# A linear-recurrence layer with two gated MLPs: the causal mask of the key products goes from VectorE to GpSimd, the low half of the receptance products from GpSimd to VectorE, and the instruction order is planned anew

## The chip, the core and the metric

One core of one Trainium2 chip runs the whole program. The time is that of one execution in microseconds (us) on the device; 1069.03 us is the median of three runs of the kernel before.

## What is computed

The reference has three parts, one behind the other. With 4 sequences, 8 heads, 768 steps and a head width of 40, each head keeps a 40x40 state:

```
for t in range(S):
    y[:, :, t] = einsum('bhd,bhde->bhe', r_t, state)
    Sa = einsum('bhde,bhe->bhd', state, a_t)
    state = state * w_t[:, :, None, :] - einsum('bhd,bhe->bhde', Sa, b_t)
    state = state + einsum('bhd,bhe->bhde', v_t, k_t)
x = y as 3072 tokens of 320
h = x @ w_in (320x2048);   g = h where h >= 1, 0 where h <= -1, else (h+1)**2/4;   x = g @ w_out
x = (silu(x @ w_gate) * (x @ w_val)) @ w_out2          (320x1536, then back to 320)
```

All inputs are float32.

## The kernel before

**Chunks.** Time is cut into 12 chunks of 64 steps. Within a chunk the recurrence is written as matrix products, one "pass" for each of the 4 sequences, so there are 48 passes. Float32 values are carried as a float16 high part and a float16 low part (value minus high part), and the products of the parts are added up in PSUM.

**A pass in front** (`p_tasks`, independent of the state): keys and receptances are scaled with the decays, split into parts (`kbs`, `ars`), turned, and multiplied at L889 (`pg`, 128 partitions x 512, the key products). The upper 64 partitions are masked causally by VectorE at L895 (PSUM times a 0/1 `mask`, into the SBUF tile `gf` for chunks 2 to 11, in place in PSUM for chunks 0 and 1), the lower 64 are copied by ScalarE at L899. From `gf` come `lkt` (high part ScalarE L910, low part GpSimd L916) and `l21` (L912, L570).

**The inverse** (`inv_tasks`, one for each chunk): 62 steps on VectorE in pairs (L955, L960), in a `pg` slot of PSUM.

**A pass behind** (`m_tasks`, needs the state of the chunk before): products at L1086, L1097, L1104, a turn by DMA, then the receptance products at L1165 into `pg`. VectorE masks them at L1171 into the SBUF tile `qf` (chunks 1 to 11), ScalarE casts the high part at L1175 into `wt`, GpSimd subtracts for the low part (helper `split`, L570). L1189 uses `wt` for y and the new state; L1195, L1198 and a DMA turn make the state of the next chunk, and L1222 makes the chunk's y, which goes by DMA to the MLPs.

**The MLPs.** For each chunk (256 tokens) layer 1 runs 8 pieces of L1234 (`ph`), ScalarE L1266/L1267, VectorE L1270, cast L1254, GpSimd low part L570, and L1301 (`po`); layer 2 runs 6 pieces with gate and value (L1234, L1281, L1284) and L1301. The weights are read during the first third in 58 pieces; VectorE takes the bits apart in three rows for each (L644, L648, L654).

**The order.** Every operation is a task with an engine, a cost and a due time. A planner (`Plan.forward`, `Plan.backward`) places the tasks in a list for each engine; engines work through their lists in order. Tables of numbers for each chunk and each step shift the due times. PSUM `pg` has two slots, shared by key products, receptance products, y and the inverse; `gf` and `qf` have one slot each. A task that writes a tile is placed only once the planner has a slot for it.

Of the kernel before, what the change touches and what calls it, by code (L numbers as in the profile page):

```python
# [8 lines left out]
F32 = mybir.dt.float32  # L9
# [3 lines left out]
ALU = mybir.AluOpType  # L13


class Plan:
# [10 lines left out]
    def __init__(self):  # L27
        self.tasks, self.made, self.pools, self.slots = [], {}, {}, {}
        self.bias, self.unit, self.nudge, self.last = 0.0, ["z", 0, 0], ({}, {}), ({}, {})
        self.lim, self.rounds, self.loose = 1.13, 4, ()  # L30
# [38 lines left out]
    def forward(self, prio):  # L69
# [59 lines left out]
        while done < len(ts):  # L129
            started = True  # L130
            while started:
                started = False
                for eng in self.ENGINES[:5]:
# [7 lines left out]
                    while any(heaps):  # L141
# [42 lines left out]
                        if t["dma"]:  # L184
                            heapq.heappush(events, (end, -1))
                            dma = max(dma, begin) + t["dma"]
                            end = dma + 1.94
                        else:
                            end += t["lat"]
# [30 lines left out]
    def backward(self, prio):  # L220
# [16 lines left out]
        def lat(t):  # L237
            return 1.44 + t["dma"] if t["dma"] else t["lat"]
# [107 lines left out]
def tile_recurrence__then__gated_mlps(  # L346
# [40 lines left out]
    WTP = range(1, 12)  # L387
# [63 lines left out]
    sbt("qf", [128, H, C], F32, 1)  # L451
# [83 lines left out]
    def c_v(n, ps=False):  # L535
        return 0.15 + n * 1.04e-3
# [19 lines left out]
    def hc(ap):  # L556
        return ap.rearrange("p (h t) -> p h t", h=H)
# [266 lines left out]
    def p_tasks(n, p):  # L824
# [61 lines left out]
        def mm():  # L886
# [8 lines left out]
        T("DVE", c_v(512, True), lambda: v_.tensor_tensor(  # L895
            out=gm(), in0=hc(G("pg", key))[0:C],
            in1=mask[0:C].unsqueeze(1).to_broadcast([C, H, C]), op=ALU.mult),
          r=[(key, "g")], w=[(key, "gm")], use=PG + GM, p=p)
        T("ACT", c_s(512), lambda: s_.activation(  # L899
            out=G("gf", key)[C:128], in_=hc(G("pg", key))[C:128], func=AF.Copy, scale=2.0**-6),  # L900
          r=[(key, "g")], w=[(key, "gf")], use=PG + GF, p=p)

# [114 lines left out]
    def m_tasks(n, p):  # L1017
# [144 lines left out]
        def mm_q():  # L1162
# [5 lines left out]
        wtp = c in WTP  # L1168
        qm = lambda: G("qf", key) if wtp else hc(G(pg, (key, "q")))
        QM = [("qf", key)] if wtp else PQ  # L1170
        T("DVE", c_v(512, True), lambda: v_.tensor_tensor(  # L1171
            out=qm(), in0=hc(G(pg, (key, "q"))),
            in1=mask.unsqueeze(1).to_broadcast([128, H, C]), op=ALU.mult),
          r=[(key, "q")], w=[(key, "pf")], use=PQ + QM, p=p)
        T("ACT", c_s(512), lambda: s_.copy(out=G("wt", key)[:, 0, :, 0:C], in_=qm()),  # L1175
          r=[(key, "pf")], w=[(key, "ph")], use=QM + WT, p=p)
        e4, eng, cost = side(wtp, 512)
        T(eng, cost, lambda: split(G("wt", key)[:, 1, :, 0:C], qm(), 1.0, G("wt", key)[:, 0, :, 0:C], e4),
          r=[(key, "ph")], w=[(key, "wt")], use=QM + WT, p=p)

# [160 lines left out]
    def by(tables):  # L1341
# [3 lines left out]
        "a": {0: 0.7, 11: -0.75},  # L1345
        "b": {3: 0.07, 5: -0.15, 7: 1.48, 8: -0.07, 10: 2.42, 11: 7.11},
        "d": {0: 5.17, 1: 4.15, 2: 3.13},
        "i": {0: -2.35, 1: -1.77, 2: -1.74, 3: -0.61, 4: 2.98, 6: 1.13, 7: 3.24, 8: 2.28, 9: 3.28, 10:
            7.81, 11: 4.67},
        "o": {0: 49.18},  # L1350
        "p": {15: 0.02, 16: 0.55, 17: 0.02, 18: 0.02, 19: 0.02, 20: 0.02},
        "v": {3: 0.77, 16: 0.81, 17: 0.81},
        "w": {0: 0.8, 1: 0.03, 2: -0.74, 3: -1.52, 4: -2.29, 5: -3.06, 6: -3.84, 7: -4.61},
        "z": {0: 16.32},
    })
    by_step = by({
# [37 lines left out]
    })  # L1394
    by_step = by({
# [179 lines left out]
```

## Time and profile before

| | |
|---|---|
| median of three runs | 1069.03 us (1068.96 to 1069.24) |
| profiled execution, its own time | 1068.32 us |
| its span, first to last instruction | 1066.6 us |
| mean granted TensorE clock | 0.978 of full |
| busy: TensorE / VectorE / ScalarE / GpSimd | 881.3 / 683.1 / 734.7 / 812.0 us |

The own time is 1.7 us above the span, and the median 0.7 us above that. A busy share is a mean over stages: before the MLPs start TensorE is mostly idle, and behind that it is hardly ever idle. So stages have to be read one by one. In the rows PE is TensorE, DVE VectorE, ACT ScalarE, POOL GpSimd.

### The profile page before, as it was taken

What the parts mean: (1) busy time and instruction counts of PE and PEld (TensorE: products, weight loads), DVE (VectorE), ACT (ScalarE), POOL (GpSimd) and SP (SyncE); (2) the same over time, 40 slices, a digit from 0 to 9 for tenths busy, and PEclk for the clock granted to TensorE, in tenths of its full rate; (3) what the DMA queues carried; (4) which work ended last, traced back from release to release, by engine and by line L of the source; (5) the groups of instructions that cost most, each with busy time, mean ns of one, the idle gap of its engine ahead of it and who ended that gap; (6) DMA issues with size and microseconds to landing.
All of it is one profiled execution on the core that took longest, in us unless ns stands there. A gap on an engine that the chain in (4) does not pass through costs nothing. (4 is left out here: it accounts for less than half of the span.)

```text
span 1066.6 us, 28811 instructions
## 1 busy us (share of the span) xinstructions
PE 881.3 (83%) x10944; PEld 730.6 (68%) x10944; DVE 683.1 (64%) x1773; ACT 734.7 (69%) x1358; POOL 812.0 (76%) x1040
## 2 busy tenths in 40 slices
PE   0322233947976999999999999999999999999998
PEld 0321232826754788888888878888888888888887
DVE  8879996896798475684855937648459467431211
ACT  1787575867976886978769779687697774653422
POOL 4589788877889799998998989999898785542221
PEclk9999999967988999999999999999999999999999
DMA  7987777688897689787768785887758454120000
GB/s 226 217 199 205 205 175 165 156 181 195 169 239 174 132 147 152 140 157 149 146 132 164 126 164 116 155 169 155 133 116 161 87 110 75 49 49 16 15 1 26
DMA packets 386195, 147.94 MB, mean 139 GB/s; under 512 B 344536, under 2 KB 362776, under 8 KB 386056
## 3 DMA queue, kind: packets, MB, share of 16 engines
q1 hardware_dynamic: 364756, 137.70, 61.1%
q10 hardware_dynamic: 21300, 8.40, 3.9%
q8 instruction: 85, 1.39, 0.6%
q14 instruction: 54, 0.44, 0.1%
HBM read 78.25 MB, written 21.52 MB: 94 GB/s over the span
## 5 line engine op out<-in xcount | busy, mean ns | idle before, releaser
L1301 PE MATMUL po<-wo,mx 128*128 128x320 f16 x2016 | 310.8, 300 | 4.2 <-POOL wo L570 2.2
L570 POOL TENSOR_TENSOR mx<-mx 128x512 f16<-128x512 f32 x168 | 194.1, 1159 | 109.9 <-ACT mx L1254 104.0
L1301 PEld LDWEIGHTS <-mx 128*128 128x128 f16 x2016 | 190.3, 98 | 71.3 <-issue 4.5
L1234 PE MATMUL ph<-mx,w 128*128 128x256 f16 x1536 | 194.1, 277 | 6.3 <-DMA mx<-x 3.5
L1234 PEld LDWEIGHTS <-w 128*128 128x128 f16 x1536 | 148.3, 99 | 29.6 <-issue 7.2
L1234 PE MATMUL ph<-x2t,wg 128*128 128x256 f16 x1152 | 142.8, 275 | 2.8 <-POOL wg L570 1.4
L1270 DVE SCALAR_TENSOR_TENSOR mx<-ph,mx 128x512 f32<-128x512 f32 x96 | 66.2, 689 | 123.2 <-ACT mx L1267 123.0
L1234 PE MATMUL ph<-x2t,wv 128*128 128x256 f16 x1152 | 141.7, 274 | 3.9 <-DVE wv L572 3.9
L1254 ACT CAST mx<-mx 128x512 f16<-128x512 f32 x168 | 102.7, 613 | 61.3 <-DVE mx L1284 31.6
L1234 PEld LDWEIGHTS <-wg 128*128 128x128 f16 x1152 | 110.5, 98 | 19.0 <-POOL wg L570 1.9
L1234 PEld LDWEIGHTS <-wv 128*128 128x128 f16 x1152 | 110.9, 98 | 18.2 <-DVE wv L572 4.2
L960 DVE TENSOR_TENSOR pg<-pg,ub 128x126 f32<-128x126 f32 (+22 forms) x372 | 96.1, 258 | 8.9
L1284 DVE SCALAR_TENSOR_TENSOR mx<-ph,mx 128x512 f32<-128x512 f32 x72 | 49.5, 688 | 78.3 <-PE ph L1234 76.9
L955 DVE SCALAR_TENSOR_TENSOR ub<-ub,pg 128x126 f32<-128x126 f32 (+22 forms) x372 | 92.1, 248 | 10.0 <-DMA ub<-lsd 0.6
L1266 ACT ACTIVATE mx<-ph 128x512 f32<-128x512 f32 x96 | 57.0, 593 | 25.4 <-PE ph L1234 20.2
L576 POOL TENSOR_TENSOR ldp<-ldp 128x640 f32<-128x640 f32 (+1 forms) x46 | 69.4, 1516 | 5.5 <-ACT ldp L856 3.4
L1281 ACT ACTIVATE mx<-ph 128x512 f32<-128x512 f32 x72 | 42.8, 595 | 41.5 <-PE ph L1234 37.8
L1129 ACT ACTIVATE vss<-px 32x640 f16<-32x640 f32 x90 | 61.6, 691 | 8.2 <-PE px L1097 5.8
L572 DVE SCALAR_TENSOR_TENSOR vss<-px,vss 32x320 f16<-32x320 f32 x90 | 43.5, 484 | 36.2 <-ACT vss L1129 32.4
L572 DVE SCALAR_TENSOR_TENSOR xs<-px,xs 32x320 f16<-32x320 f32 x88 | 42.3, 483 | 34.4 <-ACT xs L1115 32.4
L1267 ACT ACTIVATE mx<-mx 128x512 f32<-128x512 f32 x96 | 60.5, 630 | 3.0
L1097 PEld LDWEIGHTS <-tt 96*128 96x128 f16 (+1 forms) x768 | 28.2, 97 | 45.3 <-DMA tt<-tsd 24.4
(238 smaller groups left out, 1742.4 us busy)
## 6 DMA issues: line engine op xcount, KB each, us to landing
ldp<-in_ar_dram SPq DMA_DIRECT2D x21, 320.0 KB
ldp<-in_kb_dram SPq DMA_DIRECT2D x20, 320.0 KB
ldv<-in_v_dram SPq DMA_DIRECT2D x20, 320.0 KB
ub<-lsd SPq DMA_DIRECT2D x22, 256.0 KB
wo<-in_wo_dram SPq DMA_DIRECT2D x17, 320.0 KB
out_dram<-mx SPq DMA_DIRECT2D x23, 160.0 KB
ldp<-was SPq DMA_DIRECT2D x21, 160.0 KB
waf<-was SPq DMA_DIRECT2D x21, 160.0 KB
```

Source lines behind the costliest of these rows:

```text
L570: e.tensor_tensor(out=out, in0=x, in1=hi, op=ALU.subtract)
L572: e.scalar_tensor_tensor(out=out, in0=x, scalar=scale, in1=hi, op0=ALU.mult, op1=ALU.subtract)
L576: e.tensor_tensor(out=out, in0=x, in1=y, op=ALU.mult)
L955: v_.scalar_tensor_tensor(out=t, in0=L()[:, j, j + 1:].unsqueeze(1).to_broadcast([128, nm, ni]), scalar=-(2.0**-10), in1=m[:, 0:nm, j:j + ...
L960: v_.tensor_tensor(out=m[:, 0:nm, j + 1:], in0=m[:, 0:nm, j + 1:], in1=t, op=ALU.add)
L1129: s_.activation(out=hi2(G("vss", key)[z]), in_=two(hd(G("px", key))[32 * hf:32 * hf + 32]), func=AF.Copy, scale=-(2.0**-10))
L1234: t_.matmul(out=ps, lhsT=wts[:, wi, fs], rhs=xT[:, xi, :], start=(i == 0), stop=(i == len(plan) - 1))
L1254: T("ACT", c_s(512) - 0.04, lambda: s_.copy(out=G("g", key)[:, 0], in_=u2(key)), r=[(key, "u")], w=[(key, "gh")], use=U + GG, p=p)
L1266: s_.activation(out=u2(key), in_=ps2(key), func=AF.Relu, scale=2.0**-8, bias=1.0)
L1267: s_.activation(out=u2(key), in_=u2(key), func=AF.Square, scale=2.0**3)
L1270: T("DVE", c_v(512, True), lambda: v_.scalar_tensor_tensor(out=u2(key), in0=ps2(key), scalar=2.0**8, in1=u2(key), op0=ALU.max, op1=ALU.min ...
L1301: t_.matmul(out=ps, lhsT=g[:, x, f, 128 * tt:128 * tt + 128], rhs=wo[:, 2 * i + f, y, :], start=(n == 1 and f == 0 and m == 0), stop=(n == ...
```

## The change

Three things are changed.

First, for chunks 2 to 11 ScalarE copies all 128 partitions of the key products to `gf` in one instruction (L899 widened), and GpSimd sets the masked elements of the upper 64 partitions to zero in place by an index select. VectorE's mask product at L895 stays for chunks 0 and 1 only.

Second, the receptance products are masked in place in PSUM. ScalarE casts from PSUM, and VectorE subtracts from PSUM. The tile `qf` and its slot are gone.

Third, constants of the planner and all tables of due times are other numbers.

```diff
-        T("DVE", c_v(512, True), lambda: v_.tensor_tensor(
-            out=gm(), in0=hc(G("pg", key))[0:C],
-            in1=mask[0:C].unsqueeze(1).to_broadcast([C, H, C]), op=ALU.mult),
-          r=[(key, "g")], w=[(key, "gm")], use=PG + GM, p=p)
+        z = slice(0 if lkp else C, 128)
         T("ACT", c_s(512), lambda: s_.activation(
-            out=G("gf", key)[C:128], in_=hc(G("pg", key))[C:128], func=AF.Copy, scale=2.0**-6),
+            out=G("gf", key)[z], in_=hc(G("pg", key))[z], func=AF.Copy, scale=2.0**-6),
           r=[(key, "g")], w=[(key, "gf")], use=PG + GF, p=p)
+        if lkp:
+            T("Pool", c_ps(512), lambda: p_.affine_select(
+                out=gm(), in_=gm(), pattern=[[0, H], [1, C]], compare_op=ALU.is_gt, fill=0.0, base=0,
+                channel_multiplier=-1),
+              r=[(key, "gf")], w=[(key, "gm")], use=GF, p=p)
+        else:
+            T("DVE", c_v(512, True), lambda: v_.tensor_tensor(
+                out=gm(), in0=gm(), in1=mask[0:C].unsqueeze(1).to_broadcast([C, H, C]), op=ALU.mult),
+              r=[(key, "g")], w=[(key, "gm")], use=PG, p=p)
...
-        wtp = c in WTP
-        qm = lambda: G("qf", key) if wtp else hc(G(pg, (key, "q")))
-        QM = [("qf", key)] if wtp else PQ
         T("DVE", c_v(512, True), lambda: v_.tensor_tensor(
-            out=qm(), in0=hc(G(pg, (key, "q"))),
+            out=hc(G(pg, (key, "q"))), in0=hc(G(pg, (key, "q"))),
             in1=mask.unsqueeze(1).to_broadcast([128, H, C]), op=ALU.mult),
-          r=[(key, "q")], w=[(key, "pf")], use=PQ + QM, p=p)
-        T("ACT", c_s(512), lambda: s_.copy(out=G("wt", key)[:, 0, :, 0:C], in_=qm()),
-          r=[(key, "pf")], w=[(key, "ph")], use=QM + WT, p=p)
-        e4, eng, cost = side(wtp, 512)
-        T(eng, cost, lambda: split(G("wt", key)[:, 1, :, 0:C], qm(), 1.0, G("wt", key)[:, 0, :, 0:C], e4),
-          r=[(key, "ph")], w=[(key, "wt")], use=QM + WT, p=p)
+          r=[(key, "q")], w=[(key, "pf")], use=PQ, p=p)
+        T("ACT", c_s(512), lambda: s_.copy(out=G("wt", key)[:, 0, :, 0:C], in_=hc(G(pg, (key, "q")))),
+          r=[(key, "pf")], w=[(key, "ph")], use=PQ + WT, p=p)
+        T("DVE", c_v(512), lambda: split(
+            G("wt", key)[:, 1, :, 0:C], hc(G(pg, (key, "q"))), 1.0, G("wt", key)[:, 0, :, 0:C]),
+          r=[(key, "ph")], w=[(key, "wt")], use=PQ + WT, p=p)
...
-        "w": {0: 0.8, 1: 0.03, 2: -0.74, 3: -1.52, 4: -2.29, 5: -3.06, 6: -3.84, 7: -4.61},
+        "w": {0: 10.6, 1: 11, 2: 11.41, 3: 11.8, 4: 12.2, 5: 12.19, 6: 12.99, 7: 13.39},
```

Of the tables one line stands here (`w` shifts the weight pieces of layer 1); all others have other numbers too.

What the new order looks like is shown at three places. The lists of the kernel before have its line numbers, the lists of the changed kernel their own (L642, L646, L652 are a weight piece's three rows there, L1271 is layer 1's VectorE row, L1172 the mask of the receptance products, L568 the helper's subtraction).

The first place is VectorE's list just ahead of the first layer-1 row of chunk 0. Before:

```order
L895 TENSOR_TENSOR gf_119<-pg_130,mask 64x512
L644 TENSOR_SCALAR px_129<-wo_67 128x320
L648 SCALAR_TENSOR_TENSOR px_129<-wo_67,px_129 128x320
L738 RECIPROCAL wg<-wg 128x2x40
L739 TENSOR_SCALAR wg<-wg 128x2x40
L752 COPY wg<-wg 128x40
L757 COPY wg<-wg 32x40 x4
L654 SCALAR_TENSOR_TENSOR wo_67<-wo_67,px_129 128x320
L794 SCALAR_TENSOR_TENSOR wg<-wg 32x40 x4
L895 TENSOR_TENSOR gf_119<-pg_131,mask 64x512
L572 SCALAR_TENSOR_TENSOR vss_97<-px_128,vss_97 32x8x40
L572 SCALAR_TENSOR_TENSOR xs_116<-px_128,xs_116 32x320
```

Now, the same stretch:

```order
L642 TENSOR_SCALAR px_128<-wo_67 128x320
L646 SCALAR_TENSOR_TENSOR px_128<-wo_67,px_128 128x320
L652 SCALAR_TENSOR_TENSOR wo_67<-wo_67,px_128 128x320
L570 SCALAR_TENSOR_TENSOR vss_96<-px_127,vss_96 32x8x40
L570 SCALAR_TENSOR_TENSOR xs_117<-px_127,xs_117 32x320
L570 SCALAR_TENSOR_TENSOR vss_96<-px_127,vss_96 32x8x40
L736 RECIPROCAL wv<-wv 128x2x40
L737 TENSOR_SCALAR wv<-wv 128x2x40
L750 COPY wg<-wv 128x40
L755 COPY wg<-wv 32x40 x4
L792 SCALAR_TENSOR_TENSOR wg<-wg 32x40 x4
L570 SCALAR_TENSOR_TENSOR xs_116<-px_127,xs_116 32x320
```

The key masks (L895) of chunk 2 are gone from here, and rows of chunk 1's passes (`vss`, `xs`) stand there earlier. Ahead of the first layer-1 row (L1270 before, L1271 now) stand 28 first rows of weight pieces before (L644) and 23 now (L642).

The second place is VectorE's list at the receptance mask of a pass of chunk 2. Before:

```order
L1171 TENSOR_TENSOR qf_121<-pg_130,mask 128x512
L895 TENSOR_TENSOR gf_119<-pg_131,mask 64x512
L572 SCALAR_TENSOR_TENSOR vss_96<-px_128,vss_96 32x8x40
L1270 SCALAR_TENSOR_TENSOR mx<-ph_132,mx 128x512
L654 SCALAR_TENSOR_TENSOR wo_67<-lsp,px_129 64x256 x2
```

Now:

```order
L1172 TENSOR_TENSOR pg_130<-pg_130,mask 128x512
L652 SCALAR_TENSOR_TENSOR lsp<-lsp,px_128 128x512
L570 SCALAR_TENSOR_TENSOR xs_117<-px_127,xs_117 32x320
L642 TENSOR_SCALAR px_128<-wo_67 128x512
L568 TENSOR_TENSOR wt_101<-pg_130,wt_101 128x8x64
```

The mask stays in the `pg` slot, and the subtraction (L568) comes behind three other rows.

The third place is GpSimd's list at the `gf` of a pass of chunk 2. Before:

```order
L570 TENSOR_TENSOR ars_95<-ldp_112,ars_95 128x8x40
L570 TENSOR_TENSOR kbs_73<-ldp_112,kbs_73 128x8x40
L916 TENSOR_TENSOR lkt_84<-gf_119,lkt_84 64x512
L570 TENSOR_TENSOR l_90<-gf_119,l_90 32x256
L570 TENSOR_TENSOR vss_96<-ldv_113,vh_114 128x8x40
```

Now:

```order
L854 COPY ldp_112<-ldp_112 64x640
L898 AFFINE_SELECT gf_119<-gf_119 64x512
L568 TENSOR_TENSOR l_90<-gf_119,l_90 32x256
L568 TENSOR_TENSOR w_63<-wo_67,w_63 128x2x256
L574 TENSOR_TENSOR ldp_112<-ldp_112 128x2x320 x2
```

The select (L898) stands ahead of the pass's other GpSimd rows.

## Rows read from the trace of the kernel before

**Rows 1.** Page: busy time, share of the span and instructions of each engine

```profile
PE 881.3 (83%) x10944; PEld 730.6 (68%) x10944; DVE 683.1 (64%) x1773; ACT 734.7 (69%) x1358; POOL 812.0 (76%) x1040
```

**Rows 2.** Busy time by stage (from:to, length, engines, clock, DMA share, GB/s)

```profile
0.00:180.20 180.20, 42.34 (x609) 35.64 (x610) 154.59 (x427) 111.55 (x192) 132.89 (x252) 1.00 0.79 199
180.20:213.90 33.70, 33.32 (x447) 27.03 (x447) 25.98 (x75) 25.21 (x46) 29.58 (x41) 1.00 0.67 163
213.90:247.80 33.90, 12.20 (x223) 9.11 (x219) 29.61 (x62) 22.16 (x41) 24.42 (x30) 0.61 0.86 183
247.80:290.00 42.20, 41.09 (x500) 33.59 (x497) 28.15 (x54) 37.25 (x69) 34.64 (x39) 0.95 0.80 177
290.00:337.30 47.30, 32.39 (x336) 23.12 (x335) 44.26 (x118) 34.17 (x68) 42.53 (x47) 0.86 0.95 221
337.30:350.00 12.70, 11.55 (x84) 8.96 (x83) 9.02 (x28) 8.52 (x17) 11.25 (x12) 0.85 0.57 111
350.00:860.00 510.00, 505.67 (x6585) 424.36 (x6583) 320.37 (x848) 399.62 (x745) 451.74 (x532) 1.00 0.75 142
970.00:1066.60 96.60, 93.10 (x787) 76.72 (x785) 15.59 (x25) 32.92 (x59) 24.26 (x21) 1.00 0.05 16
```

**Rows 3.** Waits of PE from 350 to 1066.6 us: us, times, longest

```profile
PE pg L1189 <- ACT gf L899: 0.6, 2, 0.3
...
PE pg L1165 <- DVE ss L572: 0.2, 1, 0.2
```

**Rows 4.** Timeline of PE: first matmuls of layer 1 (chunks 0, 1, 2)

```profile
180.19 1.86 PE L1234 MATMUL ph<-mx,w 128*128 128x256 f16 x8 [3.45 <-DMA mx<-x]
...
247.83 7.60 PE L1234 MATMUL ph<-mx,w 128*128 128x256 f16 x48
...
337.26 3.62 PE L1234 MATMUL ph<-mx,w 128*128 128x256 f16 x16
```

**Rows 5.** Groups by line: the operations that are removed, moved or widened

```profile
L570 POOL TENSOR_TENSOR wt<-qf,wt 128x512 f16<-128x512 f32 x44 | 50.9, 1156 | 9.8 <-ACT wt L1175 7.8 <-DVE gf L895 0.9
...
L899 ACT ACTIVATE gf<-pg 64x512 f32<-64x512 f32 x46 | 27.2, 592 | 13.6 <-DVE gf L895 5.6 <-PE pg L889 2.8 <-POOL wo L570 1.6
L895 DVE TENSOR_TENSOR gf<-pg,mask 64x512 f32<-64x512 f32 x40 | 27.2, 680 | 19.6 <-ACT gf L899 11.9 <-PE pg L889 6.5 <-POOL xs L1120 0.7
```

**Rows 6.** Groups by line and shape: rows nearest to the added operations

```profile
L570 DVE TENSOR_TENSOR wt<-po,wt 128x512 f16<-128x512 f32 x2 | 1.4, 692 | 0.4 <-ACT wt L1175 0.3
...
L591 POOL TENSOR_SCALAR_AFFINE_SELECT eyem<-eyem 64x512 f16<-64x512 f16 x2 | 1.4, 717 | 0.1
...
L1266 ACT ACTIVATE mx<-ph 128x512 f32<-128x512 f32 x96 | 57.0, 593 | 25.4 <-PE ph L1234 20.2 <-POOL xs L1120 1.6 <-POOL mx L570 1.3
```

**Rows 7.** Groups by line: an inverse step, a pass's low part, a weight piece (VectorE)

```profile
L960 DVE TENSOR_TENSOR pg<-pg,ub 128x126 f32<-128x126 f32 (+22 forms) x372 | 96.1, 258 | 8.9
...
L572 DVE SCALAR_TENSOR_TENSOR xs<-px,xs 32x320 f16<-32x320 f32 x88 | 42.3, 483 | 34.4 <-ACT xs L1115 32.4
...
L644 DVE TENSOR_SCALAR px<-wo 128x320 int32<-128x320 int32 (+2 forms) x35 | 19.4, 553 | 0.5
...
L654 DVE SCALAR_TENSOR_TENSOR wo<-wo,px 128x320 int32<-128x320 int32 (+2 forms) x35 | 18.2, 521 | 0.6
```

**Rows 8.** Timeline of one receptance product of chunk 1: DVE, then ACT, then POOL

```profile
230.26 0.69 DVE L1171 TENSOR_TENSOR qf<-pg,mask 128x512 f32<-128x512 f32 x1
...
230.99 0.62 ACT L1175 CAST wt<-qf 128x512 f16<-128x512 f32 x1 [0.25 <-DVE qf L1171]
...
232.39 1.15 POOL L570 TENSOR_TENSOR wt<-qf,wt 128x512 f16<-128x512 f32 x1
```

**Rows 9.** Timeline of PE shortly before chunk 2's layer 1

```profile
334.02 0.46 PE L1301 MATMUL po<-wo,mx 128*128 128x320 f16 x2 [1.12 <-POOL wo L570]
335.54 0.43 PE L1301 MATMUL po<-wo,mx 128*128 128x320 f16 x1 [1.06 <-ACT wo L666]
336.77 0.69 PE L1301 MATMUL po<-wo,mx 128*128 128x320 f16 x2 [0.81 <-POOL wo L570]
```

More of the change, by code (lines that the diff above doesn't have):

```diff
@@ L29, in __init__ @@
         self.bias, self.unit, self.nudge, self.last = 0.0, ["z", 0, 0], ({}, {}), ({}, {})
-        self.lim, self.rounds, self.loose = 1.13, 4, ()
+        self.lim, self.rounds, self.loose = 1.39, 4, ()
     def pool(self, name, tiles):
@@ L186, in forward @@
                             dma = max(dma, begin) + t["dma"]
-                            end = dma + 1.94
+                            end = dma + 2.02
                         else:
@@ L237, in lat @@
         def lat(t):
-            return 1.44 + t["dma"] if t["dma"] else t["lat"]
+            return 0.87 + t["dma"] if t["dma"] else t["lat"]
         seen = set()
@@ L386, in tile_recurrence__then__gated_mlps @@
     XSP = range(12)
-    WTP = range(1, 12)
     LKP = range(2, 12)
@@ L450, in tile_recurrence__then__gated_mlps @@
     sbt("pf", [128, H, C], F32, 1)
-    sbt("qf", [128, H, C], F32, 1)
     mx = sbt("mx", [128, 36 * NT], F16)
@@ L1344, in tile_recurrence__then__gated_mlps @@
     by_chunk = by({
[L1345 to L1352, printed above, removed]
-        "w": {0: 0.8, 1: 0.03, 2: -0.74, 3: -1.52, 4: -2.29, 5: -3.06, 6: -3.84, 7: -4.61},
-        "z": {0: 16.32},
[24 rows of a table added]
     })
     by_step = by({
[12 rows of a table removed]
[14 rows of a table added]
     })
```

161 rows, old and new, of tables (by_chunk, by_step) are left out of this document.

## The prediction

> **What bounds the kernel now.** I read the busy shares first [rows 1]: TensorE is busy for 881 of 1066.6 us, and no other engine for more than 812. That is a mean over unlike stages, so the stages come next [rows 2]. From 350 to 860 us TensorE is busy for 505.7 of 510 us at full clock, and from 970 to the end for 93.1 of 96.6 us. There it sets the pace, and nothing that VectorE or GpSimd saves can shorten it. Up to 350 us it is another kernel: before layer 1 of chunk 0 begins, at 180.2 us [rows 4], TensorE works for 42 of 180 us and VectorE for 154.6. From 213.9 to 247.8 us TensorE works for 12.2 of 33.9 us at a clock of 0.61: the layer-1 work of chunk 0 is used up and chunk 1's y is not there yet. From 290 to 337.3 us it works for 32.4 of 47.3 us, while VectorE is busy for 44.3 and the DMA engines for 0.95 of the time. Chunk 2's layer 1 starts at 337.26 us [rows 4], and from about there TensorE has work without a break. So the end is the start of chunk 2's layer 1, plus what TensorE then still has to do. The second is almost the same in both kernels: counted in TensorE's lists, 272 + 192 matmuls of 256 columns and 234 of 320 stand ahead of that start before, 264 + 192 and 240 now. The change is worth what it does before 350 us.
>
> **The parts, over the whole program.** VectorE loses 40 masks of 680 ns [rows 5], 27.2 us, and gets 44 subtractions from PSUM. Chunk 0 already did this one from PSUM in 692 ns [rows 6], so they are 30.4 us: VectorE +3.2 us. GpSimd loses 44 subtractions of 1156 ns [rows 5], 50.9 us, and gets 40 selects. The nearest row is a select over the same 64x512 elements, in float16, at 717 ns [rows 6]: 28.7 us, GpSimd -22.2 us. Its bounds are 0.6 us (as short as ScalarE's one-input copy, 592 ns) and 1.16 us (a subtraction of two float32 inputs [rows 5]); I take the row of the same operation. ScalarE's copy goes from 64 to 128 partitions and costs the same, 592 against 593 ns for 128x512 [rows 5, 6]. Behind 350 us all of this lies beside TensorE: GpSimd is busy for 452 and VectorE for 320 of 510 us [rows 2]. There I cost it at nothing. If that cover were gone, GpSimd's side alone would be worth some 0.5 us a pass.
>
> [...]
>
> **The parts, before 350 us.** Here VectorE's list is what I go by, since it is busy for 283 of 337 us up to chunk 2's layer 1 [rows 2] and its rows are in order. I counted its rows ahead of three points, before and now.
> - First layer-1 row of chunk 0: 5 first and second rows of weight pieces and 6 third rows fewer, 4 masks fewer, 1 low part more. With 0.553, 0.553, 0.521, 0.680 and 0.483 us [rows 5, 7] that is -10.9 us. The weights come later: by chunk 0's last layer-1 row the list is about 7 us longer than before, since there 1 piece more, 6 low parts more, and 3 of the new subtractions stand ahead.
> - First layer-1 row of chunk 1: 4 subtractions more (+2.8), 5 masks (-3.4), 1 piece (-1.6) and 5 low parts (-2.4) fewer: -4.7 us.
> - First layer-1 row of chunk 2: 8 subtractions more (+5.5), 10 masks fewer (-6.8), and 3 inverse rows of 0.26 us [rows 7] with two small memsets fewer (-0.9): **-2.2 us**. This is the first term.
>
> Between the second and third point the list is therefore 2.5 us longer than before (-2.2 against -4.7). But VectorE is idle there for 17.1 of 89.5 us (42.2 + 47.3 less 28.2 + 44.3 [rows 2]). How much of the 2.5 us goes into that idle time no row shows; the bounds are 0 and 2.5. I take 2.0, since TensorE's order leaves room for it: chunk 1's four y come with 48, 96, 104 and 128 layer-1 matmuls ahead of them in place of 80, 128, 128 and 128, so two of the four no longer lie behind all of chunk 0's work, in the stretch in which TensorE starved. Second term: **-2.0 us**.
>
> The 58th and last weight piece stands 10 us earlier in VectorE's list than before. TensorE waits for weights of the output products for 1.12, 1.06 and 0.81 us just before chunk 2's layer 1 [rows 9], 3.0 us in all. The matmuls that waited are then still to be done. Bounds: 0 (the DMA engines, at 0.95 in that stretch, hold the loads back) and 3.0. I take -1.8, a little over half. Third term: **-1.8 us**.
>
> The receptance chain gets shorter. In one pass the mask starts at 230.26, the cast ends at 231.61 and GpSimd's low part ends at 233.54 [rows 8]; VectorE could end it near 232.4. It lies beside other work as soon as another sequence's pass is ready; I cost it at nothing, at most 1.1 us for each of chunk 1's last passes.
>
> Sum: -2.2 - 2.0 - 1.8 = -6.0 us. The span goes from 1066.6 to 1060.6 us, the profiled execution's own time from 1068.32 to 1062.3 us, and the median, 0.7 us above that, to **1063.0 us**.
>
> **Rivals.**
> *The gap is filled much better.* VectorE is idle for 12.0 us between 180.2 and 247.8 us (67.6 less 26.0 + 29.6) and for 17.1 between 247.8 and 337.3 [rows 2]. If the new order uses half of these 29.1 us, chunk 2 starts 14.5 us earlier; with the first and third terms that is -18.5, 1050.5 us. For it speaks that y is moved so far forward; against it, that DMA is at 0.8 to 0.95 there and its bytes stay.
>
> *No change.* VectorE's list to chunk 2 is shorter by only 2.2 us, 0.2% of the time. If the idle time takes nothing and the weights come no earlier, the time is 1066.8 us, or anything up to 1071 where a wait comes anew.
>
> *Slower, by the PSUM slot.* The mask now stays in the `pg` slot until cast and subtraction are done: from 230.95 to about 232.4 in the pass of rows 8, so 1.45 us longer in each of 44 passes. The inverse holds one of the two slots for a long time, and key products, y and receptance products share the other; TensorE's list is in order, so a product without a slot holds back the layers behind it. Today TensorE waits for `pg` to come free only 0.6 and 0.2 us behind 350 us [rows 3], which speaks against it. If 0.3 us of the 1.45 reached TensorE in each pass, it would be +13.2 us, 1076 us with the -6.0. It decides from 0.14 us a pass on (6.0 / 44).
>
> *Slower, by late weights.* Chunk 0's layer 1 ends later by the 7 us that its list is longer. If that carries through to chunk 2 in place of the second and third terms, with half of it lost, it is +3.5 - 2.2 + 2: about 1072 us.
>
> *A slow select.* GpSimd has 58 us free from 350 to 860 us [rows 2], in which some 28 selects fall. They use it up when each takes 2.1 us (58 / 28) more than the row's 717 ns; at twice that, 4.2 us more, they add 59 us, 1128 us. Against it speaks the row, the same operation over as many elements. [...]
>
> **Chances and range.** The forecast, 1057 to 1066.8 us, gets 0.48; the better filling 0.17; no change 0.16; the PSUM slot 0.11; late weights 0.07; the slow select 0.01. A measurement of this kernel can tell about 0.2% (2.1 us) from no change. So faster is 0.48 + 0.17 = 0.65, same 0.16, slower 0.19. For 8 times in 10 I keep the forecast, no change, late weights and somewhat over half of the better filling: 1052 to 1073 us. The likeliest case's own range is 1057 to 1066.8 us.
>
> **What would show it.** In the changed kernel's profile: layer 1 of chunk 0 starts some 5 to 11 us before 180, chunk 1's near 243, chunk 2's near 333; the stretch between the first and second of these shows TensorE at a higher clock than 0.61; GpSimd is busy for about 790 us and VectorE for about 686; the select's row is near 0.72 us. The forecast is wrong if TensorE's idle time from 350 to 860 us is well over 4.3 us (the slot), if chunk 2's layer 1 starts at 337 or later (no gain ahead), or before 325 (the better filling).

## The result, and the profile after

The changed kernel took **1074.71 us** (median of three runs, 1073.87 to 1076.59) against 1069.03: ratio 1.0054, 95% interval 1.0040 to 1.0067. Run once more (h0 below), 12 runs of it against 35 of the kernel before, it was 1071.17 against 1069.65 us: 1.0020, 1.0006 to 1.0035. So the change made the kernel slower, by 0.2% to 0.5%; I had forecast 1063.0 us and a range up to 1073. The second measurement lies inside that range, but on the slow side of the kernel before. The profiled execution took 1076.59 us, the longest of the three, with a span of 1074.6 us: it shows the loss larger than usual.

The page's busy times and the rows of the changed operations, as [rows 1, 5, 6]:

```profile
PE 885.6 (82%) x10944; PEld 732.6 (68%) x10944; DVE 679.7 (63%) x1777; ACT 728.5 (68%) x1358; POOL 784.6 (73%) x1036
```

```profile
L568 DVE TENSOR_TENSOR wt<-pg,wt 128x512 f16<-128x512 f32 x44 | 30.2, 686 | 6.5 <-ACT wt L1176 6.0
L898 POOL TENSOR_SCALAR_AFFINE_SELECT gf<-gf 64x512 f32<-64x512 f32 x40 | 26.1, 652 | 9.9 <-ACT gf L894 8.8
L894 ACT ACTIVATE gf<-pg 128x512 f32<-128x512 f32 x40 | 23.7, 592 | 11.5 <-issue 4.5 <-PE pg L887 4.0 <-DMA ldp<-was 2.1
```

The operations cost what was forecast, the select even less, and GpSimd has 27 us less to do. The stages show where the time went. Windows as in [rows 2] (length, busy PE, PEld, DVE, ACT, POOL, clock, DMA share):

```profile
0.00:180.20 180.20, 46.92 (x667) 38.53 (x668) 141.96 (x406) 107.86 (x185) 128.29 (x247) 1.00 0.84 194
180.20:213.90 33.70, 24.64 (x360) 19.69 (x358) 29.22 (x78) 26.95 (x50) 30.55 (x46) 0.90 0.83 192
213.90:247.80 33.90, 24.57 (x266) 18.67 (x265) 29.84 (x75) 24.57 (x47) 24.48 (x28) 0.85 0.95 191
247.80:290.00 42.20, 34.85 (x434) 27.26 (x432) 35.88 (x69) 34.84 (x68) 31.71 (x39) 0.92 0.83 194
290.00:337.30 47.30, 32.99 (x386) 25.84 (x384) 40.73 (x103) 34.16 (x68) 41.01 (x48) 0.89 1.04 196
350.00:860.00 510.00, 500.97 (x6519) 419.33 (x6517) 316.13 (x844) 392.62 (x742) 438.17 (x533) 1.00 0.76 143
```

Ahead of 350 us the starving stretch (213.9 to 247.8 us) is better filled, 24.6 us of work against 12.2, at a clock of 0.85 and not 0.61; but the stretch ahead of it (180.2 to 213.9 us) falls from 33.3 to 24.6 us. From 350 to 860 us, where I had counted on TensorE being busy as before, it does 66 matmuls fewer and is idle for 9.0 us instead of 4.3. The first matmuls of layer 1 for chunks 0, 1 and 2, as [rows 4], from the timeline of PE:

```profile
177.49 1.87 PE L1235 MATMUL ph<-mx,w 128*128 128x256 f16 x8 [0.38 <-DMA mx<-x]
...
238.32 5.12 PE L1235 MATMUL ph<-mx,w 128*128 128x256 f16 x32
...
336.50 1.04 PE L1235 MATMUL ph<-mx,w 128*128 128x256 f16 x8
```

They come 2.7, 9.5 and 0.8 us earlier than before. And the waits of PE from 350 us to the end, as [rows 3] (us, times, longest):

```profile
PE ph L1235 <- DMA mx<-x: 4.1, 2, 2.6
PE pg L1169 <- DVE ss L570: 1.7, 3, 0.8
PE ph L1235 <- DVE mx L1285: 1.2, 3, 0.5
PE pg L887 <- DVE pg L964: 0.7, 1, 0.7
PE px L1101 <- DMA tt<-tsd: 0.5, 1, 0.5
PE pg L1190 <- DVE wt L568: 0.2, 1, 0.2
```

The longest group is new: layer 1 waits for `x`, a chunk's y on its way through the turn by DMA. Before, TensorE waited for no x behind chunk 2. The two places in the timeline of PE:

```profile
557.64 2.78 PE L1235 MATMUL ph<-mx,w 128*128 128x256 f16 x24 [1.44 <-DMA mx<-x]
...
701.31 5.32 PE L1235 MATMUL ph<-mx,w 128*128 128x256 f16 x32 [2.63 <-DMA mx<-x]
```

These are chunks 5 and 7. The second wait costs twice: the 32 matmuls behind it took 5.3 us where such a group takes 3.6, and the windows there (701.3 to 704.0 and 704.0 to 706.7 us) show a granted clock of 0.65 and 0.72, each a mean of stretches at 1.00 and at 0.50 (in windows of 0.4 us it is 1.00 from 701.3 to 701.7 us, 0.50 from 702.1 to 705.3 and 1.00 again from 705.7). Behind the first wait no time was lost in this way: 24 matmuls took 2.78 us, the usual time.

**Where the lead goes.** I counted TensorE's work done by a time: every matmul begun, at its usual time (0.109 us for 256 columns, 0.136 for 320, 0.029 for 64, 0.025 for 40, 0.107 for a turn of 128, the medians from begin to begin in the kernel before; 836.1 us in all, in every run). Ahead (+) or behind (-) the profiled execution of the kernel before, in us of work, for one profiled execution each of the changed kernel (result and second run) and of kernels from the experiments:

| at us | 340 | 350 | 540 | 680 | 720 | 860 | 1060 |
|---|---|---|---|---|---|---|---|
| changed kernel | +2.7 | +0.3 | +0.4 | -0.9 | -5.3 | -7.8 | -7.3 |
| changed kernel, second run (h0) | +3.0 | +2.5 | +0.6 | +0.2 | -0.5 | -2.5 | -2.3 |
| two loads later (h1) | +4.6 | +5.1 | +4.8 | +5.2 | +4.4 | +2.4 | +2.9 |
| the same kernel, run again (k0) | +3.7 | +3.9 | +0.2 | +0.9 | +0.1 | -1.9 | -1.5 |
| the two loads on SP's queue (k1) | +1.7 | +2.6 | -0.7 | +0.4 | -1.1 | -2.8 | -2.3 |
| two loads and two products later (k2) | +3.7 | +3.6 | +2.3 | +4.1 | +4.0 | +1.8 | +2.3 |
| six transfers later (f57) | +3.7 | +3.3 | +3.2 | +3.0 | +3.2 | 0.0 | +0.5 |
| kernel before, one turn moved (g7) | -0.4 | -0.9 | -1.0 | -1.1 | -1.4 | -1.3 | -1.4 |

The changed kernel is ahead when chunk 2's layer 1 starts and loses that lead, and more, in a stretch that I had costed at nothing. One row is one execution: h1 and k0 are the same kernel and end 4.4 us apart. The profiled executions of h1, k2 and f57 are among the three shortest of their 12; those of h0 and k0 are near their medians.

**Why x is late.** The issues on SP's queue and on ScalarE's around chunk 7's second turn of x (L1017 in the changed kernel, L1013 before). Changed kernel:

```profile
693.26 0.60 SPq L1042 DMA_DIRECT2D waf<-was  x1
693.96 1.31 SPq L1017 DMA_TRANSPOSE mx<-x  x1
695.38 1.28 SPq L805 DMA_TRANSPOSE kbT<-kbs  x1
696.71 4.17 SPq L805 DMA_TRANSPOSE art<-ars  x1
...
694.20 0.38 ACTq L836 DMA_DIRECT2D ldp<-in_ar_dram  x1
```

Kernel before:

```profile
692.04 1.25 SPq L1013 DMA_TRANSPOSE mx<-x  x1
693.34 1.30 SPq L807 DMA_TRANSPOSE kbT<-kbs  x1
694.73 1.35 SPq L807 DMA_TRANSPOSE art<-ars  x1
696.13 0.60 SPq L843 DMA_DIRECT2D ldp<-wks  x1
696.79 0.66 SPq L838 DMA_DIRECT2D ldp<-in_ar_dram  x1
```

Before, the load of 320 KB for a later pass stands behind x in the same queue, and x's matmuls start 5.64 us after the issue without a wait. Now ScalarE issues it, 0.24 us after x, and x lands 7.35 us after its issue (693.96 to 701.31). At chunk 5 it is 6.90 us, and there ScalarE issues such a load 1.90 us ahead of x (548.84 against 550.74 us). The planner put more such loads there; issues on ScalarE's queue from 350 to 860 us (KB each), before and after:

```profile
ldp<-in_ar_dram ACTq DMA_DIRECT2D x1, 320.0 KB
```

```profile
ldp<-in_ar_dram ACTq DMA_DIRECT2D x7, 320.0 KB
```

### The profile page after: what moved, and what is told of

Read it like the earlier page. It is cut to its first block, busy times and chain, and to the rows that moved or that the text cites. A ratio compares the mean times of both kernels' runs of the same rounds, so it can differ in the third digit from the quotient of the medians.

```text
span 1074.6 us, 28752 instructions
## 1 busy us (share of the span) xinstructions
PE 885.6 (82%) x10944; PEld 732.6 (68%) x10944; DVE 679.7 (63%) x1777; ACT 728.5 (68%) x1358; POOL 784.6 (73%) x1036
## 4 chain that ended last, share of the span: by engine, by line
PE 48%; DVE 20%; ACT 10%; POOL 7%; DMA 7%; issue 5%; SPq 1%; ACTq 0%; POOLq 0%; DVEq 0%
PE ph L1235 25%; PE po L1302 17%; DVE pg L964 3%; DVE ub L959 3%; PE pg L1190 2%; DMA mx<-x 2%; POOL mx L568 1%; PE px L1090 1%; DVE vss L570 1%; DVE px L642 1%; ACT vss L1133 1%; DVE xs L570 1%; DVE px L646 1%; DMA ub<-lsd 1%; PE px L1101 1%
## 5 line engine op out<-in xcount | busy, mean ns | idle before, releaser
L568 POOL TENSOR_TENSOR mx<-mx 128x512 f16<-128x512 f32 x168 | 193.9, 1156 | 120.2 <-ACT mx L1255 115.2
L1271 DVE SCALAR_TENSOR_TENSOR mx<-ph,mx 128x512 f32<-128x512 f32 x96 | 66.1, 689 | 123.8 <-ACT mx L1268 123.1
L1124 POOL COPY xs<-xs 32x320 f16<-32x320 f16 x94 | 41.8, 446 | 23.0 <-ACT xs L1119 18.4
```

The lines of the kernel that those rows point to most:

```text
L568: e.tensor_tensor(out=out, in0=x, in1=hi, op=ALU.subtract)
L1271: T("DVE", c_v(512, True), lambda: v_.scalar_tensor_tensor(out=u2(key), in0=ps2(key), scalar=2.0**8, in1=u2(key), op0=ALU.max, op1=ALU.min ...
```

## The experiments

Line numbers in kernels made from the changed one are up to 4 higher. "Ratio" is to the kernel before on the same chip; single runs of one kernel spread there over up to 11.6 us (k2), so where ratios overlap I go by the traces.

**e1, e2, e3, e4: which part, operations or order?** The planner writes the lists, so an edit normally moves everything. In e1 to e3 the lists were kept and only what a task issues was exchanged; e4 plans the new operations with the old tables and constants.

e1, slot of the receptance products freed early:

```diff
+        qm = lambda: qfs[0] if c else hc(G(pg, (key, "q")))
-            out=hc(G(pg, (key, "q"))), in0=hc(G(pg, (key, "q"))),
+            out=qm(), in0=hc(G(pg, (key, "q"))),
```

> The changed kernel with its own lists, row for row; only the receptance mask of chunks 1 to 11 writes an SBUF tile (qf) again, and cast and subtraction read that, so the pg slot comes free at the mask's end and not at the subtraction's. Slot theory: TensorE's waits for pg (0.69, 0.73 and 0.79 us at 602, 676 and 796 us) and what follows from them go, 1069 to 1071 us. Order theory (the new lists bring x too late to the MLPs): 1074 to 1075 us, as the changed kernel, with the waits for x at 557 and 701 us still there. Operations theory (the select on GpSimd delays the passes): 1074 to 1075 us too.

e2, in the same lists the old operations too (subtraction on GpSimd; at the widened copy's place VectorE's mask and the narrow copy):

```diff
-            G("wt", key)[:, 1, :, 0:C], qm(), 1.0, G("wt", key)[:, 0, :, 0:C]),
+            G("wt", key)[:, 1, :, 0:C], qm(), 1.0, G("wt", key)[:, 0, :, 0:C], p_ if c else v_),
```

> The changed kernel's lists with the old operations in them: VectorE masks the key products of chunks 2 to 11 from PSUM where the widened copy stood, no select, the receptance products go to qf, and GpSimd subtracts. Order theory: the time stays near the changed kernel's, 1074 to 1078 us (GpSimd has 22 us more to do in a list made for less), waits for x remain. Operations theory and slot theory: the operations of before bring back 1068 to 1071 us.

e3, the lists of before with the new operations:

```diff
+                s_.activation(
+                    out=G("gf", key), in_=hc(G("pg", key)), func=AF.Copy, scale=2.0**-6)
+                p_.affine_select(
+                    out=gm(), in_=gm(), pattern=[[0, H], [1, C]], compare_op=ALU.is_gt, fill=0.0, base=0,
+                    channel_multiplier=-1)
...
-        T(eng, cost, lambda: split(G("wt", key)[:, 1, :, 0:C], qm(), 1.0, G("wt", key)[:, 0, :, 0:C], e4),
+        T(eng, cost, lambda: split(G("wt", key)[:, 1, :, 0:C], qm(), 1.0, G("wt", key)[:, 0, :, 0:C]),
```

> The lists of the kernel before with the new operations in them: one copy of all 128 partitions and the select where mask and copy stood, the receptance mask still into qf, the subtraction on VectorE from qf. Order theory: not slower than before, 1066 to 1070 us, as the operations alone cost TensorE nothing. Operations theory: 1073 to 1076 us. Slot theory says nothing against 1069 us here, since qf takes the product out of pg.

e4: the changed kernel with `lim` 1.13, 1.94, 1.44 and all tables of before.

> The changed operations with the planner constants and due-time tables of the kernel before, so the planner makes a third order. Order theory: anything between 1065 and 1090 us, since no table was made for these tasks; if it is below 1072 us, the new tables are the loss. Operations or slot theory: 1074 us or more, since the operations are the changed kernel's.

Measured (4 or 5 runs each, 9 of before): e1 1085.58 us, ratio 1.0144 (1.0124 to 1.0165); e2 1094.18, 1.0234 (1.0212 to 1.0255); e3 1093.80, 1.0228 (1.0211 to 1.0246); e4 1098.21, 1.0265 (1.0251 to 1.0279). Nearly every time that was expected was missed (in e2 the waits for x did remain, 4.1 us in three). Old operations in the new lists and new operations in the old lists both cost 2.3%. So neither "the order" nor "the operations" is the loss by itself. I read it so: a list fits the durations for which it was searched, and exchanging either side costs more than the whole change. e2 shows how, in PE's waits from 340 us (times and longest behind the sum): the subtraction, again 1156 ns on GpSimd, comes late nine times for the product that makes y (L1196 in e2).

```profile
PE pg L1196 <- POOL wt L569: 5.4, 9, 0.9
```

e1 and e3 don't tell what they were made for, since they changed a duration too. The group of the subtraction in e1, then in e3:

```profile
L569 DVE TENSOR_TENSOR wt<-qf,wt 128x512 f16<-128x512 f32 x44 | 46.8, 1064 | 6.9 <-ACT wt L1178 6.5
```

```profile
L570 DVE TENSOR_TENSOR wt<-qf,wt 128x512 f16<-128x512 f32 x44 | 41.3, 938 | 5.5 <-ACT wt L1190 5.1
```

From an SBUF tile it takes 1064 and 938 ns, from PSUM 686. In e1 that is 16.6 us more on VectorE, and the kernel is 10 to 13 us slower than the changed one (1.0144 against its two ratios), although VectorE is busy for 64%. The longest of these subtractions in e1 took 3247 ns, the shortest 674; no run isolates the cause.

**f5, f7, f57, g7: is it x?** Here only DMA issues are moved; every engine's other work stays in its place. In the planned program order, task i goes right behind task j:

```diff
+        for i, j in self.behind:
+            x = next(o for o in order if o[0] == i)
+            order.remove(x)
+            order.insert([o[0] for o in order].index(j) + 1, x)
...
+    K.behind = [(2479, 2085), (2149, 2085), (2476, 4785), (2996, 5053), (2997, 5053), (3072, 5053)]
```

These are the six moves of f57 (2085 is chunk 5's turn of x, 4785 and 5053 the first layer-1 matmuls of chunks 5 and 7, 2476 and 3072 loads on ScalarE's queue); f5 has the first three, f7 the last three.

> The changed kernel, all lists as they are but for three DMA issues: the turn of one key part (art of pass 31) and one load of pass 32's decays go behind chunk 5's second turn of x in SP's queue, and one load of pass 32 on ScalarE's queue goes behind the first layer-1 matmul of chunk 5. Late-x theory (x waits behind other transfers in the DMA queues): the wait of 1.44 us at 557 us shrinks to under 0.5, time 1 to 1.5 us below the changed kernel's 1074.7, so 1073.2 to 1073.7 us. Rival (x is late because GpSimd and VectorE finish it late): the wait stays over 1.2 us, 1074.7 us.

> The changed kernel with three DMA issues moved at chunk 7: two loads of decays for pass 34, which stand directly ahead of the second turn of x, and one load for pass 40 on ScalarE's queue go behind the first layer-1 matmul of chunk 7. Late-x theory: the wait of 2.63 us at 701 us falls below 1.6 us, and with it some of the 1.7 us that the 32 matmuls behind it took longer at the lower clock: 1071.5 to 1073.5 us. Rival (the producers of x are late): 1074.7 us.

> Both sets of moves in one kernel. Late-x theory: the gains add up, 1070 to 1072.5 us, and at 720 us the changed kernel is about as far as the kernel before. Rival: 1074.7 us, with the time lost elsewhere behind 700 us.

g7 is the kernel before with `K.behind = [(2773, 2837)]`.

> The kernel before with one DMA issue moved: chunk 7's second turn of x goes behind the two turns (kbs of pass 38, ars of pass 39) that follow it in SP's queue, as the changed kernel has such turns ahead of it. Late-x theory: TensorE, which waits for no x behind 350 us in the kernel before, now waits there for 2 to 4 us and loses some clock, 1071.5 to 1075 us. Rival (turns ahead of x cost nothing): 1069.0 us.

Measured (12 runs each, 35 of before at 1068.74): f5 1070.17, ratio 1.0021 (1.0005 to 1.0036); f7 1070.36, 1.0011 (0.9999 to 1.0023); f57 1070.67, 1.0019 (1.0002 to 1.0035); g7 1068.64, 0.9985 (0.9967 to 1.0003). Each wait for x went at the chunk at which the issues were moved: f5 waits 0.8 us once (chunk 7), f7 1.2 us once (chunk 5), f57 not at all. The ratios are below 1.0054 but too close to the 1.0020 of the second measurement to show a gain; f57, without any wait for x, has 1.0019. g7 went against the theory as I had put it: with two turns ahead of it in SP's queue, x of chunk 7 still landed within 2.7 us of its issue. So turns ahead of x are not what holds it up, and f7 had moved two things at once.

**h0 to h3: which queue?**

> The changed kernel as it is, once more and with more runs, as the measure for the three kernels beside it. All theories: a ratio to before near 1.0054, waits for x at about 557 and 701 us.

h1: `K.behind = [(2476, 4785), (3072, 5053)]`, the two loads on ScalarE's queue alone.

> The changed kernel with only the two 320 KB loads on ScalarE's DMA queue moved (for passes 32 and 40, behind the first layer-1 matmul of chunks 5 and 7); SP's queue as in the changed kernel. Second-queue theory (these loads share the DMA engines with the turn of x and make it land late): both waits for x under 0.8 us, ratio 1.001 to 1.003. Rival (the SP transfers ahead of x in its own queue are what delays it): waits for x of 1 to 2.6 us remain, ratio 1.004 to 1.006.

h2: the other four moves alone.

> The changed kernel with only the four transfers in SP's queue moved behind x (a turn of ars and a load ahead of chunk 5's x, two loads ahead of chunk 7's x); the loads on ScalarE's queue stay. Second-queue theory: x is issued up to 1.3 us earlier but still takes about 7 us to land, the waits shrink by no more than that, ratio 1.003 to 1.005. Own-queue theory: waits under 0.8 us, ratio 1.001 to 1.003.

h3, in the kernel before:

```diff
+    K.behind = [(3074, 2836), (3072, 2836)]
...
+            order.insert([o[0] for o in order].index(j) + 1, (i, "ACT"))
```

> The kernel before with two 320 KB loads of pass 40 taken from SP's queue, where they stand four and six places behind chunk 7's second turn of x, to ScalarE's queue, so that they can start 2 to 3 us after the turn is issued. Second-queue theory: x of chunk 7 lands later than the 5.64 us that it has at most, TensorE waits 0.5 to 2 us at about 698 us, ratio 1.0005 to 1.003. Own-queue theory: no wait there, ratio 1.000.

Measured (12 runs each, 35 of before at 1069.65): h0 1071.17, ratio 1.0020 (1.0006 to 1.0035); h1 1068.94, 1.0002 (0.9986 to 1.0019); h2 1070.41, 1.0008 (0.9993 to 1.0022); h3 1071.24, 1.0012 (0.9997 to 1.0027). PE's waits from 350 us in h0 still hold x; in h1 the list has these groups above 0.2 us and x is gone:

```profile
PE ph L1235 <- DMA mx<-x: 1.1, 2, 0.6
```

```profile
PE pg L1173 <- DVE ss L574: 1.6, 3, 0.7
PE ph L1239 <- DVE mx L1289: 1.2, 3, 0.5
PE pg L1194 <- DVE wt L572: 0.9, 2, 0.7
PE pg L1173 <- DVE ub L574: 0.4, 1, 0.4
```

In h1 chunk 7's layer 1 starts 3.88 us after the turn's issue, not 7.35 (SP's queue, then PE):

```profile
689.47 1.31 SPq L1021 DMA_TRANSPOSE mx<-x  x1
...
693.35 1.91 PE L1239 MATMUL ph<-mx,w 128*128 128x256 f16 x16
```

In the times, h0 and h1 ran on the same chip, 12 runs each: h1's median is 2.2 us lower (95% by resampling these runs: 0.4 to 5.2), and that is more than h0's 1.1 us of waiting for x.

h2 waits for no x at chunks 5 and 7 either, which speaks for the other theory: at chunk 7 the load on ScalarE's queue is issued 0.81 us after x, and x still lands within 4.91 us. So both count: with both, x took 7.35 us (5.64 in h0); with the load moved at most 3.88; with the two loads ahead of it moved at most 4.91. Either is enough to end the wait. This holds in every profile of the changed lists: where neither was moved TensorE waits for x (chunk 5: 1.44, 0.60 and 1.15 us in the result, h0 and f7; chunk 7: 2.63, 0.51 and 0.83 in the result, h0 and f5), and where either was moved it does not. h3 looks from the other side: in the kernel before, with the two loads on ScalarE's queue (695.54 and 696.93 us), the turns right behind them become late. The state's turn on SP's queue, which takes 1.21 us to issue in the kernel before, and PE's new wait:

```profile
700.04 5.83 SPq L1208 DMA_TRANSPOSE s0t<-ss  x1
```

```profile
PE pg L1169 <- DMA vsT<-vss: 1.1, 1, 1.1
```

By the count of work, h3 falls from 1.6 us behind the kernel before at 680 us to 4.3 at 720. It was not x that waited, as I had expected, but another turn.

**k0 to k3: queue or bytes, and the slot.**

> The changed kernel with the two loads on ScalarE's queue behind chunk 5's and 7's first layer-1 matmuls, as run before, as the measure for the three kernels beside it: no waits for x at chunks 5 and 7, ratio 0.999 to 1.002.

k1, k2 and k3:

```diff
+        order = [(i, "SP" if i in (2476, 3072) else eng) for i, eng in order]
...
+    K.behind = [(2476, 4785), (3072, 5053), (2368, 4879), (3277, 5237)]
...
+        order = [(i, "SP" if self.tasks[i]["eng"] == "DQ" else eng) for i, eng in order]
```

> The changed kernel with the same two loads at their own places in the program, but issued from SP's queue instead of ScalarE's, where they stand behind x. Queue theory (a second queue lets the load's packets run beside the turn that was issued first): x lands within 6 us, waits for x at chunks 5 and 7 under 0.5 us, ratio 0.999 to 1.002. Rival (the bytes of the load at that moment delay x from either queue): waits for x of 0.6 to 2.6 us as in the changed kernel, ratio 1.002 to 1.005.

> As the first kernel of this call, and two receptance products (passes 27 and 37), which wait 0.5 to 0.8 us each for a pg slot, stand one TensorE task later. Slot theory: these two waits go and nothing new comes, 1 to 1.4 us less than the first kernel, ratio 0.998 to 1.001. Rival (the passes are late by as much next): the waits go, the time stays.

> The changed kernel with all transfers that ScalarE issues issued from SP at the same places (37 in the program order of ScalarE, 69 counted as tasks; SP then carries all 811). Queue theory: no turn is overtaken, waits for x, kbT and tt behind 350 us under 0.6 us in sum, ratio 0.998 to 1.002. Rival: SP, which issues one after the other at 0.3 to 1.3 us each, becomes late itself, ratio 1.003 to 1.01.

Measured (12, 12, 12 and 9 runs, 32 of before at 1069.55): k0 1070.04, ratio 1.0007 (0.9994 to 1.0021); k1 1068.98, 0.9998 (0.9983 to 1.0012); k2 1068.74, 1.0001 (0.9982 to 1.0020); k3 1071.84, 1.0029 (1.0015 to 1.0043). k1 speaks for the queue and against the bytes: the same load is issued 1.42 us behind x from SP's queue, and x's matmuls start 3.91 us after x's issue, without a wait. It doesn't settle it alone, since the load also starts later than in the changed kernel (1.42 us behind x and not 0.24; at chunk 5, 2.08 us behind it and not 1.90 ahead):

```profile
694.94 1.32 SPq L1018 DMA_TRANSPOSE mx<-x  x1
696.36 0.52 SPq L837 DMA_DIRECT2D ldp<-in_ar_dram  x1
...
698.85 1.36 PE L1236 MATMUL ph<-mx,w 128*128 128x256 f16 x11
```

k2: two of the waits for a `pg` slot are gone; what k0 shows as 1.8 us is here

```profile
PE pg L1173 <- DVE ss L574: 0.2, 1, 0.2
```

and no other group is over 0.2 us longer than in k0; the times of k0 and k2 can't be told apart. k0 itself waits for no x, and still loses 3.4 us of work between 400 and 420 us, at another thin place (its rows):

```profile
407.73 0.74 ACT L870 ACTIVATE ars<-ldp 128x640 f16<-128x640 f32 x1 [2.36 <-DMA art<-ars]
...
408.60 0.79 POOL L572 TENSOR_TENSOR ars<-ldp,ars 128x320 f16<-128x320 f32 x1 [3.01 <-ACT ars L870]
409.35 1.16 POOL L572 TENSOR_TENSOR mx<-mx 128x512 f16<-128x512 f32 x1
...
410.56 0.72 PE L1306 MATMUL po<-wo,mx 128*128 128x320 f16 x4 [1.87 <-POOL mx L572]
...
411.56 3.16 PE L1239 MATMUL ph<-mx,w 128*128 128x256 f16 x16
```

By the profile ScalarE waits until a turn by DMA has read `ars`, GpSimd waits for ScalarE, its next row is the low part that layer 1 needs, and TensorE waits 1.87 us for that. The 16 matmuls a little later took 3.16 us, where 1.91 is usual. TensorE waits at this place, 0.7 to 1.9 us, in six of the eleven profiles of the changed lists (h0, h2, f5, k0, k1, k2), and in none of the three with the lists of before (the kernel before, g7, h3). No experiment touched it.

k3: x waits nowhere, but SP becomes late itself, and PE waits for the turns of keys from 340 us on:

```profile
PE pg L888 <- DMA kbT<-kbs: 2.5, 1, 2.5
PE px L1102 <- DMA tt<-tsd: 2.1, 3, 1.1
```

So putting everything on SP's queue is no cure; what mattered for x was the load beside a turn on which TensorE waits: x of chunk 7 took 5.64 us to land with the load beside it in another queue (h0), and at most 3.91 with the load behind it in its own (k1). How the load holds x up, no run shows. No version beats the kernel before by more than its interval.

## Why the prediction was wrong

**The step that failed** is "Behind 350 us all of this lies beside TensorE", and "There I cost it at nothing", with the sentence that the end is the start of chunk 2's layer 1 plus what TensorE then still has to do. From 350 to 860 us the changed kernel lost 8.1 us of work against the kernel before in the profiled run and 5.0 in h0's. In the profiled run 4.1 us of that are the two waits for x and 1.7 the clock behind the second one. The remaining 2.3 are the balance of more waiting for `pg` slots (1.1, and 0.7 for a slot that the inverse held), less waiting elsewhere, and gaps too short for the list; no experiment took them apart. That transfers placed beside and ahead of x cause the waits for x is shown by h1 and h2, with k1.

That x is most of what the change costs is not shown. The profiled run is the longest of its three; h0, near its median, waits only 1.1 us for x. And the six profiled kernels with the changed lists that wait for no x from 350 us on (h1, h2, f57, k0, k1, k2) still lose 1.8 to 6.5 us from 350 to 860 us, 4.3 in the mean; g7, with the lists of before, loses 0.4. So the new order has more thin places than one, k0's at 410 us among them, and TensorE, with 1 to 2% to spare, covers none of them.

The engines' busy shares, on which I argued, could not show this; the issues on each queue could have shown x's part. In the order I had followed VectorE's, GpSimd's and TensorE's lists, and not ScalarE's DMA issues behind 350 us, 7 loads of this kind there against 1.

**The terms ahead of 350 us** (-2.2, -2.0, -1.8) had, taken together, the right sign and over twice the size. In the ten profiled kernels whose lists agree up to there TensorE is ahead by 0.1 to 4.6 us at 340 us, 2.8 in the mean, and by -0.4 to 5.1 at 350, 2.4 in the mean; in the result's own profile only 0.3 us are left at 350, after two more waits (1.10 and 1.32 us) and 16 matmuls at the lower clock. Chunk 0 came 2.7 us earlier and not 5 to 11; chunk 1, at 238.3, much earlier than the 243 I named; and chunk 2 at 336.5 where I had 333. The count of matmuls ahead of chunk 2's start was misread, too: 272 and 264 take in chunk 2's own first group; by the trace it is 256 + 192 of 256 columns in both kernels, and 234 and 240 of 320, so the changed kernel has 0.6 us of work less to do from there. Between chunks 1 and 2 the lead was given back, against the second term: TensorE works 67.8 us from 247.8 to 337.3, 73.5 before, and VectorE 76.6 against 72.4. The DMA engines are at 1.04 from 290 to 337 us, 0.95 before. The third term (weights earlier) came to nothing: TensorE waits for them just as long at the end of the stretch, 1.85 and 1.10 us, as in [rows 9]; its lower bound, 0, was the one to take; whether the DMA engines held the loads back, no run shows.

```profile
335.42 1.25 PE L1302 MATMUL po<-wo,mx 128*128 128x320 f16 x8 [1.85 <-POOL wo L568]
...
342.04 0.43 PE L1302 MATMUL po<-wo,mx 128*128 128x320 f16 x2 [1.10 <-POOL wo L568]
```

**The operations** were sized right: select 652 ns (717 taken), subtraction 686 (692), copy 592 (593). GpSimd ended 27.4 us lower, not 22.2, and VectorE 3.4 lower, not 3.2 higher, as other rows changed with the order.

**The rivals.** Slower by the `pg` slot would have needed 0.14 us a pass; TensorE waits 1.9 us at receptance and y products (1.7 and 0.2, 0.04 us a pass, against 0.8 before), most of it until a row that makes the state has let go of a slot, so it is real and small, and k2 took two of its waits away without a gain that could be measured. Late weights, better filling and a slow select did not happen. What was seen, transfers that land late and in-order lists that pass the delay on, was not among my rivals.

**What stays open:** what the three operations are worth under an order searched equally well for both. e2 to e4 show that an order that doesn't fit hides it behind 2.3 to 2.7%. How much of the loss is x's stays open as well. For it: h1, k0, k1 and k2, without waits for x, have ratios of 0.9998 to 1.0007, and h1 is 2.2 us below h0 on one chip. Against it: f57, without them too, has 1.0019, and k0's trace loses as much behind 350 us as h0's (5.8 against 5.0). The waits in the traces carry the argument on x, the times don't carry it.

## What to carry to other kernels

When a planner writes the order anew, read its DMA issues on each queue as closely as its engines' lists, above all beside a transfer on which the busy engine waits: here a load of 320 KB on a second queue, issued 0.24 us after x in the result's profile, was not behind it: x took 7.35 us to land, and at most 3.91 with the load 1.42 us behind it in its own queue (k1). TensorE, busy for 98% of the time (501.0 of 510 us), was not a cover for everything here: x, 2.63 us late at chunk 7, cost these 2.63 us and then 1.7 us at the lower clock. And compare several profiles of each kernel before putting a loss of 5 us down to one wait: two traces of one kernel ended 4.4 us apart here. And a searched order was worth more here (2.3 to 2.7% in e2 to e4) than the edit that it was searched for, so a saving of 0.5% by operations can't be forecast without looking at the new order's thinnest places.

## What the runs showed of the hardware

- A DMA turn of x took 6.90 (chunk 5) and 7.35 us (chunk 7) to land beside a 320 KB load on another queue in the result's profile, 6.11 and 5.64 in h0's, and at most 5.29 and 3.91 us with that load behind it in its own queue (k1).
- VectorE's subtraction of 128x512 float32 reads PSUM in 686 ns, of 44 none above 692. From SBUF the same took 674 to 3247 ns, median 922 (e1), while GpSimd was busy for 74% of the time.
- A wait of 2.63 us was followed by 5.4 us at a granted clock of 0.65 and 0.72, which cost 1.7 us more; behind one of 1.44 us the 24 matmuls ran at their usual pace.
